# A gated attention and feed-forward decode kernel: the first weight matrix sent as eight transfers of sixteen rows

## The chip, the cores and the metric

The kernel runs on one core of a Trainium2 chip. The metric is the device time of one launch in microseconds. A core has five engines that matter here: TensorE (PE, with its weight loads shown as PEld), VectorE (DVE), ScalarE (ACT), GpSimd (POOL) and SyncE (SP), and sixteen DMA engines that move data between HBM and the on-chip memory SBUF. Data transfers are issued as instructions by SyncE and by ScalarE, each of which has a queue of its own; in the profile SyncE's is q1 and ScalarE's is q10. A transfer is cut into rows, one for each SBUF partition, and the rows are shared out over the DMA engines.

## The reference

Two tokens (batch 2, one position) of width 512 go through an attention block over a cache of 4096 positions and through a small feed-forward block; a gate mixes the two.

```python
x = A_x                                                   # [2, 1, 512]
g = sigmoid((x * gate_w).sum(-1, keepdims=True))
# attention: 32 heads of 128, K and V cache [2, 32, 4096, 128], bf16
q = (x @ wq)                                              # wq [512, 4096]
p = softmax(q k^T * 128 ** -0.5)                          # per head
a = (p v) @ wo                                            # wo [4096, 512]
# feed-forward
b = relu(x @ w1) @ w2                                     # w1 [512, 1376], w2 [1376, 512]
return g * a + (1 - g) * b
```

Everything is in bf16. The K cache and the V cache are 67 MB each; wq and wo are 4 MB each, w1 and w2 1.4 MB each.

## The kernel before, in words

The kernel is a list of instructions per engine, written out by hand. `sp(...)`, `act(...)`, `pe(...)`, `dve(...)` and `pool(...)` append one instruction to that engine's list together with what it waits for: `waits` names markers that other engines signal, `dwaits` names semaphores of transfers with the value to reach. A transfer adds 16 to its semaphore when all of it has landed. `emit` (lines 77 to 92) turns the lists into instructions, waits first.

*Where the data lies.* A large buffer `kv` has three regions (`NREG`) of 32,768 bf16 in each of 128 partitions. K and V are each cut into eight units of 8 MB; a unit fills one region, 64 KB in each partition. The units are sent in a fixed order (lines 185 to 188): five K units, then V and K by turns, then the remaining V. Each unit goes into the region that the unit three places before it has left, so from the fourth unit on SyncE waits, before it issues, for TensorE to be done with that earlier unit (lines 237 to 251). The third region first holds the small weights: wq (32 KB in each partition), w1 behind it (11,008 B in each partition: partition p holds rows 4p to 4p+3 of the matrix, which lie together in HBM), an identity matrix, and x with gate_w (lines 155 to 159). The third K unit is therefore sent only when the projection of x is done (the marks pe_qh, dve_setup and act_q).

*The first transfers.* ScalarE issues x and gate_w (lines 233 and 234), SyncE issues w1 and wq (235 and 236) and then the K units (250). The w1 transfer has 128 rows, one for each partition.

*The work behind them.* `gate` (line 282) transposes x and gate_w on TensorE and makes the gate's factors on ScalarE and VectorE. `x_proj` (line 340) waits for wq and w1 together (line 371) and multiplies x by both; its results are q, and the hidden layer before its ReLU. For each K unit VectorE transposes the region in place (`k_turn`, line 397) and TensorE multiplies by the block of queries that GpSimd has made (`w_block`, 388). `sm_max`, `sm_exp` and `sm_turn` make the softmax of a batch of four units; `spread` (442) puts the weights of one V unit in place on GpSimd, `v_go` (455) hands TensorE a token when the unit has landed, and `v_extract` (462) takes the result out. These loops run on TensorE as real loops with registers (`main_loop`, 476).

*The end.* Behind the last V unit SyncE issues w2 (line 252) and wo in four parts (255), so these are the last to arrive. ScalarE sends a rest of w2, `w2_lo`, 96 rows of 1 KB, between two V units (663). `project_first` multiplies the hidden layer by w2, `project` (615) the attention result by wo as its parts land; a copy on VectorE and one on ScalarE take the result to SBUF, and SyncE stores it (257).

*Fillers and the split of the lists.* `fill(name, n)` (609) appends n instructions that only add to a semaphore nobody waits for; they lengthen an engine's instruction list. Line 688 puts five of them on ScalarE, between the last small result and the final copy. Line 700 says how many instructions of each engine's list are emitted before TensorE's list, the rest after it: for SyncE four (w1, wq and two K units), for ScalarE two (x and gate_w).

Of the kernel before, what the change touches and what calls it, by code (L numbers as in the profile page):

```python
# [94 lines left out]
def bass_gated_mix__gqa_block_cached__dense_activation_relu__decode_kernel(  # L95
# [61 lines left out]
    w1_sb = kv[:, C, 16384:21888]  # L157
# [16 lines left out]
    def psf(p0, p1, c0, n):  # L174
        return PSF[p0:p1, c0:c0 + n]
# [4 lines left out]
    sem = {n: nc.alloc_semaphore("sem_" + n) for n in names}  # L180
# [16 lines left out]
    def freed(what):  # L197
        kind, u = what
        return f"pesc_{u}" if kind == "k" else f"pe_v_{u}"

    def sp(fn, waits=(), dwaits=()):
        P.add("sp", fn, waits=waits, dwaits=dwaits)
# [4 lines left out]
    def dve(fn, waits=(), signal=None, dwaits=()):  # L207
        P.add("dve", fn, waits=waits, signal=signal, dwaits=dwaits)

    def act(fn, waits=(), signal=None, dwaits=()):  # L210
        P.add("act", fn, waits=waits, signal=signal, dwaits=dwaits)

    def pe(fn, waits=(), signal=None, dwaits=()):
        P.add("pe", fn, waits=waits, signal=signal, dwaits=dwaits)
# [17 lines left out]

    act(lambda e: e.dma_start(x_sb[0:2], A_x.rearrange("b s d -> (b s) d")).then_inc(sem["x"], 16))
    act(lambda e: e.dma_start(x_sb[2:3], gate_w.rearrange("(o d) -> o d", o=1)).then_inc(sem["gw"], 16))
    sp(lambda e: e.dma_start(w1_sb, B_w1.rearrange("(p t) f -> p (t f)", t=4)).then_inc(sem["w1"], 16))
    sp(lambda e: e.dma_start(wq_sb, A_wq.rearrange("(p t) n -> p (t n)", t=4)).then_inc(sem["wq"], 16))
    for n, what in enumerate(order):
        if n >= NREG:
            waits = [freed(order[n - NREG])]
        else:  # L240
            waits = ["pe_qh", "dve_setup", "act_q"] if n == C else []
        if what == ("v", 7):
            c0 = 0
            for i, k in enumerate(LASTV):
                c1 = c0 + k * 4096
                sp(lambda e, n=n, c0=c0, c1=c1, i=i: e.dma_start(kv[:, n % NREG, c0:c1], unit_in(("v", 7))[:, c0:c1]).then_inc(sem["v7" + "ab"[i]], 16),
                   waits=waits if i == 0 else [])
                c0 = c1
        else:
            sp(lambda e, n=n, what=what: e.dma_start(kv[:, n % NREG, :], unit_in(what)).then_inc(sem_reg[n % NREG], 16),  # L250
               waits=waits)
# [50 lines left out]
    def r_(e, name):  # L302
        if name not in reg:
            reg[name] = e.alloc_register(name)
        return reg[name]

    def by_reg(e, ap, name):
        x = e.lower_ap(ap)
        n = reg[name].name
        return mybir.RegisterAccessPattern(ap=x.ap, dtype=x.dtype, memsetref=x.memsetref, regref=n, is_regloc_offset=False,  # L310
                                           reg_ap_offset=n, const_ap_offset=0, const_sub_tensor_id=0)

    def mm(e, dst, lhsT, rhs, cols=128, at=0, load=True):
        return e.add_instruction(mybir.InstMatmult(  # L314
            name=nc.get_next_instruction_name(), engine=mybir.EngineType.PE, ins=[rhs, lhsT], outs=[e.lower_ap(dst)],
            start_tensor_calc=False, stop_tensor_calc=False, tile_size=(128, cols), tile_position=(0, at),
            bass_skip_group_check=True, ldweights=load))

    def clear(e, dst, n, stop=False):
        return e.matmul(dst, lhsT=nil, rhs=nil.unsqueeze(1).to_broadcast([32, 4, 128]) if n == 512 else nil[:, 0:n],  # L320
                        start=not stop, stop=stop, tile_position=(0, 0), skip_group_check=True)

    def addresses(e, base, offs, first):
        for k, o in enumerate(offs):
            e.reg_add(r_(e, f"a{first + k}"), r_(e, base), o)
# [4 lines left out]
    def enter(name, parent=None, engines=(mybir.EngineType.PE,)):  # L330
        parent = nc.bb_map[parent] if parent else nc.cur_bb
        if open_block:
            open_block.pop().__exit__(None, None, None)
        b = nc.body(name, parent=parent, valid_engines=list(engines))
        b.__enter__()
        open_block.append(b)
# [3 lines left out]
    def x_proj():  # L340
        wqv = wq_sb.rearrange("p (t u a x) -> p t a u x", t=4, u=4, a=4)
        place_of = [(96 + r, 10, 128) for r in range(10)] + [(0, 1, 96)]

        def fn(e):
            for half in range(2):
                clear(e, psf(0, 128, V_C0 + BANK * half, BANK), 512)
            clear(e, psf(0, 128, H_C0, 2 * NF), 2 * NF)
            e.reg_mov(r_(e, "rm"), at["kv"] + 2 * C * REG)
            e.reg_mov(r_(e, "rh"), at["kv"] + 2 * (C * REG + 16384))
            e.reg_mov(r_(e, "rw"), at["zero"] + 4 * 636)  # L350
            e.reg_mov(r_(e, "p"), 0)
            e.br("x_pass")
            enter("x_pass")
            addresses(e, "rm", [2 * (256 * a + 2048 * half) for a in range(4) for half in range(2)], 0)
            addresses(e, "rw", [2 * 31], 8)
            addresses(e, "rh", [2 * (row + (m - 1) * n) for row, n, m in place_of], 9)
            for a in range(4):
                for half in range(2):
                    mm(e, psf(32 * a, 32 * a + 32, V_C0 + BANK * half, BANK), by_reg(e, xT32[:, 0, :], "a8"),
                       by_reg(e, wqv[:, 0, a, 2 * half:2 * half + 2, :], f"a{2 * a + half}"), 32, 32 * a, load=not half)  # L360
            for ft, (row, n, m) in enumerate(place_of):
                mm(e, psf(0, m, H_C0 + 2 * ft, 2), by_reg(e, w1_sb[:, row:row + (m - 1) * n + 1:n], f"a{9 + ft}"),
                   by_reg(e, xT32[:, 0, 0:2], "rw"))
            e.reg_add(reg["rm"], reg["rm"], 2 * 4096)
            e.reg_add(reg["rh"], reg["rh"], 2 * DFF)
            e.reg_add(reg["rw"], reg["rw"], 2 * 32)
            e.reg_add(reg["p"], reg["p"], 1)
            e.br_lt(reg["p"], 4, on_true="x_pass", on_false="x_done")
            enter("x_done")
            return clear(e, psf(0, 128, H_C0, 2), 2, stop=True)  # L370
        pe(fn, dwaits=[(sem["wq"], 16), (sem["w1"], 16)], waits=["act_xT"], signal="pe_qh")
        qt = ptm[:].rearrange("p x c h -> p (x c h)").bitcast(f32)
        dve(lambda v: v.transpose(out=qt.rearrange("p (n q) -> p n q", q=32).rearrange("p (y e) q -> p y e q", e=2),  # L373
                                  in_=PSF[:, V_C0:V_C0 + 1024].rearrange("p (y q e) -> p y e q", q=32, e=2)),
            waits=["pe_qh"], signal="dve_qt")
        act(lambda a: a.activation(out=q_sb[:].rearrange("p b u h k -> p b (u h k)"),
                                   in_=qt.rearrange("p (n x) -> p x n", x=32)[:, 0:2], func=ACT.Copy),
            waits=["dve_qt"], signal="act_q")
# [191 lines left out]
    def busy(n):  # L570
        pe(lambda e: mm(e, psf(0, 128, V_C0, n), e.lower_ap(X2[:, 0:128]), e.lower_ap(X2[:, 0:n])))
# [37 lines left out]
    def fill(name, n, dwaits=()):  # L609
        if name not in P.fill:  # L610
            P.fill[name] = nc.alloc_semaphore("fill_" + name)
        for i in range(n):
            P.add(name, lambda e: e.sem_inc(P.fill[name], 1), dwaits=(dwaits if i == 0 else ()))
# [30 lines left out]
    hint_here()  # L644
    gate()
    x_proj()
    w_block(0)
    w_block(1)
# [36 lines left out]
    busy(256)  # L685
    o_place()
    busy(512)
    fill("act", 5)
    fill("dve", 3)
    fill("pool", 3)  # L690
    fill("pool", 4, [(sem["wo2"], 16)])
# [5 lines left out]

    P.resolve()

    rest = (("sp", nc.sync, 4), ("act", nc.scalar, 2), ("pool", nc.gpsimd, 4), ("dve", nc.vector, 0))  # L700
    for name, eng, n in rest:
        P.emit(name, eng, 0, n)
    P.emit("pe", nc.tensor)
# [31 lines left out]
```

## Time and profile before

| | us |
|---|---|
| median of 3 runs | 342.68 (342.61 to 342.92) |
| the profiled execution | 342.64 |
| its span, first to last event of the profile | 341.3 |
| busy: TensorE, VectorE, GpSimd, ScalarE | 209.9, 155.4, 41.8, 13.9 |
| DMA packets, of these under 512 B | 3580, 405 |
| w1, issue to landing | 5.8 |
| wq, issue to landing | 15.0 |
| K units, issue to landing, median | 35.4 |

Times in the profile are microseconds from the start of the span. The time of an execution is 1.3 us longer than its span; forecasts are made for the time. In the DMA row of the page each digit is the mean busy share of the sixteen DMA engines in one of forty slices, in tenths, 9 for 90% or more. In the chain of waits one reads, in order of time, the work that the end waited for. In a timeline a name with q behind it (SPq, ACTq) is an engine's issue of a transfer; the number behind the start is how long the issue took, or, for several in one line, how long they took with the gaps between them. A transfer's packets are its rows, and for each DMA engine that it used one more of 4 bytes that counts up the semaphore. On q1 the rows of all its transfers are 3074 and the 4-byte packets 386, together the 3460 of the queue table.

### The profile page before, as it was taken

To read this page: it belongs to the slowest core of one execution; us is meant where nothing else is said; L and a number is where in the kernel's file an instruction comes from. 1 tells how busy PE (TensorE), PEld (TensorE's weight loads), DVE (VectorE), ACT (ScalarE), POOL (GpSimd) and SP (SyncE) were. 2 spreads that over 40 slices of the span, in tenths; PEclk is the share of its full clock that TensorE was granted. 3 is DMA by queue.
4 is the path that set the end of the run, shared out by engine and by line. 5 is a ranking of instruction groups with operands and counts; after the bars stand their busy time and mean duration, and the time that the engine had idled before them with its cause. 6 is when DMAs were issued, how large, how long until landed. Compare 5 with 4: busy or idle time off the path is not lost. (4 is left out here: it accounts for less than half of the span.)

```text
span 341.3 us, 3101 instructions
## 1 busy us (share of the span) xinstructions
PE 209.9 (61%) x1243; PEld 33.9 (10%) x843; DVE 155.4 (46%) x45; ACT 13.9 (4%) x37; POOL 41.8 (12%) x53
## 2 busy tenths in 40 slices
PE   0080079685968909972995059820993773718387
PEld 0040011000100101110111001100100100101024
DVE  1010897979799769229800693019805000000111
ACT  2001000000000020000000000000003000000000
POOL 1000000000000004005002300050000235050400
PEclk9999999999898965996799559965696659676789
DMA  8998989898999999998989898989999999999896
GB/s 346 434 492 369 492 369 492 369 492 369 492 392 468 399 461 445 415 484 376 492 369 492 369 492 369 492 369 492 392 468 392 468 438 424 398 441 461 374 440 264
DMA packets 3580, 145.46 MB, mean 426 GB/s; under 512 B 405, under 2 KB 634, under 8 KB 762
## 3 DMA queue, kind: packets, MB, share of 16 engines
q1 hardware_dynamic: 3460, 145.33, 98.7%
q10 hardware_dynamic: 118, 0.10, 0.1%
q8 instruction: 1, 0.02, 0.0%
q14 instruction: 1, 0.01, 0.0%
HBM read 145.43 MB, written 0.00 MB: 426 GB/s over the span
## 5 line engine op out<-in xcount | busy, mean ns | idle before, releaser
L404 DVE STREAM_TRANSPOSE kv<-kv 128x8192 uint32<-128x8192 uint32 (+1 forms) x17 | 138.6, 8186 | 74.4 <-DMA kv<-in_A_k_cache_dram 74.4
L314 PE MATMUL PS<-kv,zero 128*128 (+1 forms) x544 | 130.3, 421 | 40.4 <-PEq L481 40.4
L314 PE MATMUL PS<-kv,ptw 128*32 x512 | 48.1, 469 | 11.7 <-issue 11.5
L320 PE MATMUL PS<-zero 32*128 32x512 bf16 (+2 forms) x21 | 9.7, 537 | 57.6 <-ACT zero L410 20.3
L449 POOL TENSOR_TENSOR ptw<-E,mask 128x512 bf16<-128x512 bf16 x32 | 32.2, 1038 | 21.1 <-PE PS L314 10.9
L467 DVE TENSOR_TENSOR X<-PS,maskc 128x512 f32<-128x512 f32 x2 | 1.4, 692 | 64.1 <-PE PS L314 64.1
L314 PEld LDWEIGHTS PS<-kv,zero 128*128 (+1 forms) x144 | 13.6, 103 | 154.6 <-issue 154.6
L393 POOL TENSOR_TENSOR zero<-q_sb,mask 128x32 bf16<-128x32 bf16 x8 | 1.9, 251 | 147.0 <-PE PS L314 123.3
L471 POOL TENSOR_TENSOR X<-X,maskc 128x512 f32<-128x512 f32 x6 | 6.2, 1039 | 109.2 <-ACT X L470 109.2
L314 PE MATMUL PS<-X,zero 128*64 128x512 f32 x16 | 11.6, 819 | 12.3 <-PEq L481 12.3
L314 PEld LDWEIGHTS PS<-kv,ptw 128*32 x512 | 8.7, 99 | 50.4 <-issue 49.7
L320 PEld LDWEIGHTS PS<-zero 32*128 32x128 bf16 x21 | 2.1, 109 | 69.4 <-issue 43.7
L373 DVE STREAM_TRANSPOSE ptw<-PS 128x1024 f32<-128x1024 f32 x1 | 1.3, 1251 | 16.4 <-PE PS L320 16.4
L415 DVE TENSOR_REDUCE zero<-PS 128x2 f32<-128x2048 f32 x2 | 4.5, 2271 | 9.1 <-PE PS L314 9.1
L470 ACT ACTIVATE X<-PS 128x512 f32<-128x512 f32 x6 | 3.6, 597 | 71.4 <-PE PS L314 71.4
L422 ACT ACTIVATE nrow<-mmax 128x32 f32<-128x32 f32 x2 | 0.5, 228 | 132.8 <-DVE mmax L419 132.8
L440 DVE STREAM_TRANSPOSE E<-E 128x2048 bf16<-128x2048 bf16 x2 | 4.6, 2300 | 2.4 <-ACT E L430 2.4
L410 ACT ACTIVATE zero<-zero 1x1 f32<-1x1 f32 x9 | 1.8, 200 | 84.9 <-DMA kv<-in_A_v_cache_dram 67.9
L430 ACT ACTIVATE E<-PS,negm 128x1024 bf16<-128x1024 f32 x4 | 4.4, 1109 | 0.6 <-DVE negm L426 0.6
L284 PE MATMUL PS<-kv 3*128 3x3 bf16 x4 | 0.3, 165 | 6.5 <-DMA kv<-in_gate_w_dram 6.5
L598 PE MATMUL PS<-kv,oW 128*2 128x256 bf16 x64 | 4.0, 272 | 0.4 <-DMA kv<-in_A_wo_dram 0.4
L314 PEld LDWEIGHTS PS<-X,zero 128*64 (+1 forms) x16 | 1.8, 161 | 15.8 <-issue 15.6
(49 smaller groups left out, 27.6 us busy)
## 6 DMA issues: line engine op xcount, KB each, us to landing
kv<-in_A_v_cache_dram SPq DMA_DIRECT2D x1, 6144.0 KB, 36.7
kv<-in_A_wq_dram SPq DMA_DIRECT2D x1, 4096.0 KB, 15.0
kv<-in_A_wo_dram SPq DMA_DIRECT2D x1, 2560.0 KB, 35.9
kv<-in_A_v_cache_dram SPq DMA_DIRECT2D x1, 2048.0 KB, 41.3
kv<-in_B_w_dram SPq DMA_DIRECT2D x1, 1376.0 KB, 5.8
kv<-in_B_w_dram SPq DMA_DIRECT2D x1, 1280.0 KB, 30.1
kv<-in_A_wo_dram SPq DMA_DIRECT2D x1, 1024.0 KB, 37.9
kv<-in_A_wo_dram SPq DMA_DIRECT2D x1, 384.0 KB, 38.4
```

Source lines behind the costliest of these rows:

```text
L314: return e.add_instruction(mybir.InstMatmult(name=nc.get_next_instruction_name(), engine=mybir.EngineType.PE, ins=[rhs, lhsT], outs=[e.low ...
L320: return e.matmul(dst, lhsT=nil, rhs=nil.unsqueeze(1).to_broadcast([32, 4, 128]) if n == 512 else nil[:, 0:n], start=not stop, stop=stop, ...
L393: pool(lambda g: g.tensor_tensor(out=out, in0=q, in1=msk, op=ALU.mult), waits=([["act_q", "dve_mask8"], []] + [[f"pesc_{x}"] for x in rang ...
L404: ins = v.transpose(out=reg[:, 4096 * p0:4096 * p1], in_=reg[:, 4096 * p0:4096 * p1])
L410: return lambda a: a.activation(out=tick[:, 2 + i:3 + i], in_=tick[:, 0:1], func=ACT.Copy).then_inc(sem["go"], n)
L415: dve(lambda v: v.tensor_reduce(out=mpad[:, 0:2], in_=PSF[:, 0:2048].rearrange("p (x h q) -> p h x q", h=2, q=16), axis=AX.XY, op=ALU.max) ...
L430: act(lambda a, h=h: a.activation(out=E[:].rearrange("p (x h q) -> p h x q", h=2, q=16)[:, h], in_=PSF[:, 0:2048].rearrange("p (x h q) -> ...
L440: dve(lambda v: v.transpose(out=E[:], in_=E[:]), waits=[f"act_exp{b}"], signal=f"dve_et{b}")
L449: pool(lambda g, src=src, dst=dst: g.tensor_tensor(out=dst, in0=src, in1=msk, op=ALU.mult), waits=(([f"dve_et{b}"] if ub == 0 else []) + ( ...
L470: act(lambda e: e.activation(out=X2[:], in_=src, func=ACT.Copy), waits=[f"pe_v_{v}"], signal=f"act_x_{v}")
L471: pool(lambda e: e.tensor_tensor(out=X, in0=X, in1=msk, op=ALU.mult).then_inc(sem["xg"], 1), waits=[f"act_x_{v}"] + ([] if v else ["dve_se ...
L598: pe(lambda e, g=g: e.matmul(psf(64 * g, 64 * g + 2, FIN_C0, 256), lhsT=w, rhs=m[:, 256 * g:256 * g + 256], start=start, stop=stop, tile_p ...
```

## The change

w1 is sent as eight transfers in place of one. Transfer j takes the partitions j, j+8, j+16 and so on: sixteen rows of 11,008 B, one for each DMA engine. SyncE issues j = 0, 1, 3, 5 and 7, ScalarE j = 2, 4 and 6, behind x and gate_w. All eight count on the same semaphore, so TensorE now waits for 8 x 16 = 128. SyncE's wq and K units come behind its five transfers. ScalarE has three fillers fewer near the end, as many as it has transfers more. The split of the lists moves with the added instructions: eight of SyncE's and five of ScalarE's are emitted first.

```diff
     act(lambda e: e.dma_start(x_sb[2:3], gate_w.rearrange("(o d) -> o d", o=1)).then_inc(sem["gw"], 16))
-    sp(lambda e: e.dma_start(w1_sb, B_w1.rearrange("(p t) f -> p (t f)", t=4)).then_inc(sem["w1"], 16))
+
+    for j in range(8):
+        (act if j in (2, 4, 6) else sp)(lambda e, j=j: e.dma_start(w1_sb[j:128:8], B_w1.rearrange("(p t) f -> p (t f)", t=4)[j:128:8])
+                                        .then_inc(sem["w1"], 16))
     sp(lambda e: e.dma_start(wq_sb, A_wq.rearrange("(p t) n -> p (t n)", t=4)).then_inc(sem["wq"], 16))
...
-        pe(fn, dwaits=[(sem["wq"], 16), (sem["w1"], 16)], waits=["act_xT"], signal="pe_qh")
+        pe(fn, dwaits=[(sem["wq"], 16), (sem["w1"], 128)], waits=["act_xT"], signal="pe_qh")
...
-    fill("act", 5)
+    fill("act", 2)
...
-    rest = (("sp", nc.sync, 4), ("act", nc.scalar, 2), ("pool", nc.gpsimd, 4), ("dve", nc.vector, 0))
+    rest = (("sp", nc.sync, 8), ("act", nc.scalar, 5), ("pool", nc.gpsimd, 4), ("dve", nc.vector, 0))
```

## The prediction

> **What bounds the kernel.** I read the page's head and its row of DMA shares first, then the queue table, then the chain that ended last, then the timeline of the first 17 us, and at last the packet records of the trace, in which each DMA packet has a start, a duration, a size and a queue.
>
> ```profile
> span 341.3 us, 3101 instructions
> DMA  8998989898999999998989898989999999999896
> GB/s 346 434 492 369 492 369 492 369 492 369 492 392 468 399 461 445 415 484 376 492 369 492 369 492 369 492 369 492 392 468 392 468 438 424 398 441 461 374 440 264
> q1 hardware_dynamic: 3460, 145.33, 98.7%
> q10 hardware_dynamic: 118, 0.10, 0.1%
> HBM read 145.43 MB, written 0.00 MB: 426 GB/s over the span
> ```
>
> The sixteen DMA engines are busy in every slice; SyncE's queue (q1) alone holds 98.7% of their span. No engine of the core comes near (PE 61%, VectorE 46%). Packet by packet, each engine writes rows back to back: a 65,536 B row every 2.414 us in the K and V units, an 11,008 B row of w1 every 0.41 us. 145.43 MB over 16 engines at 65,536 B per 2.414 us is 334.9 us: nearly the whole span. So the kernel is one gapless stream per DMA engine, and whatever an engine loses at the start is still missing at the end, unless a gap later takes it up.
>
> ```profile
> 299.62 0.43 SPq L255
> 300.10 37.89 DMA kv<-in_A_wo_dram
> 337.99 0.04 issue
> 338.03 1.64 PE PS L598 x24
> 339.69 0.41 DVE ptw L623
> ```
>
> These are the last pieces of the chain of waits (start, length, what). The wo transfers are issued at 299.62 and wait 38 us behind what is already queued; only the last 24 matmuls, a copy and the output store stand behind the stream. The order of issue has room everywhere: the K and V units land no sooner than 24.7 us after their issue (the view of line 250) and need 8 rows x 2.414 = 19.3 of it on the engines, so at least 5.4 us of cover lie between an issue and its first row. There is no gap that could take up a loss, and none that a gain could open.
>
> ```profile
> 0.74 0.40 SPq L235 DMA_DIRECT2D kv<-in_B_w_dram  x1
> 0.74 0.54 ACTq L233 DMA_DIRECT2D kv<-in_A_x_dram  x1
> 1.19 0.42 SPq L236 DMA_DIRECT2D kv<-in_A_wq_dram  x1
> 1.31 0.23 ACTq L234 DMA_DIRECT2D kv<-in_gate_w_dram  x1
> 1.65 24.77 SPq L250 DMA_DIRECT2D kv<-in_A_k_cache_dram  x3
> 2.47 1.28 ACT L287 ACT_TABLE_LOAD   x1 [2.47 <-POOL zero L265]
> 6.53 0.26 PE L284 MATMUL PS<-kv 3*128 3x3 bf16 x4 [6.53 <-DMA kv<-in_gate_w_dram]
> 8.02 0.20 ACT L297 ACTIVATE gm<-gb 128x2 f32<-128x2 f32 x1 [0.23 <-DVE gb L296]
> 16.25 0.13 PEld L320 LDWEIGHTS PS<-zero 32*128 32x128 bf16 x2 [9.00 <-issue]
> ```
>
> This is the timeline of the start (start, length, what, idle before). The packet records beside it: w1's first rows start between 1.77 and 2.73 us on the sixteen engines and nine of them take 0.78 to 1.36 us in place of 0.41 (median over the sixteen 0.87); the second rows are nearly steady, the rest run at 0.413. The engines finish their eight rows between 5.58 and 6.13. Eight rows at 0.41 from 1.77 would end at 5.06, so this ramp costs the quickest engine 0.52 us and the slowest 1.07. The half microsecond between engines is still there in the landings of the last wo transfer (338.81 to 339.29). That ramp is all that a better start can win.
>
> **The change part by part, against the profiled execution's 342.64 us (its span 341.3 and 1.34 around it; the median of the runs shown is 342.68, 0.04 more).**
>
> SyncE issues five pieces, then wq and the K units. Issues on it follow each other by 0.45 us (0.74, 1.19, 1.65; four wo issues in 1.86). So wq goes out at about 0.74 + 5 x 0.45 = 3.0 in place of 1.19, k0 at 3.45, k1 at 3.9. From issue to first packet took 1.03 us (0.74 to 1.77): wq is on the engines at about 4.0, and they reach it no sooner than 5.06. Cost 0, covered by 1.0 us; k0 is needed at 15.27. The third K unit waits for q at 26.4 in any case, and its rows come after k1's, past 50 us.
>
> ScalarE issues three pieces behind gate_w, each some 0.35 us (line 663's issue; 0.23 and 0.54 on the two here): 1.57 to about 2.7. Its table load slips from 2.47 to 2.7 and has until 6.83. gate_w, now served at 5.60 behind seven w1 rows of its engine, has fewer rows ahead and may land some 2 us sooner; the gate's chain then ends before 8.02, and TensorE waits for wq until 16.25 anyway. Worth 0 either way, covered by 8 us.
>
> The pieces themselves: with both queues the last is issued at about 2.6 and is there at 3.6; an engine wants its eighth row at 4.64 at the earliest. Seven more semaphore packets per engine at 0.009 us: 0.06. Where an engine alternates between the two queues, w2_lo is the nearest row: with its 1 KB rows between them, the 64 KB rows take 2.447 against 2.420, so 0.027 for a switch, at most six: 0 to 0.16, and I take 0 because a switch lies beside waiting writes. One wait on 128 in place of 16 ends with the same last row. ScalarE's three fewer fillers stand in a stretch where it idles 5.2 us: 0. SyncE's four more instructions shift its code; nothing in the trace prices that, and I bound it by one issue (0.33) on either side and take 0.
>
> What is left is the price of a row, and here placement changes: a piece's sixteen rows go to every eighth partition, and all pieces take them in the same order. No row of the trace has this placement. From below: 0.41, the steady row, and no ramp: ends at 5.06, 1.07 us sooner. From above: every row costs the median first row, 0.872, from the late starters' 2.42: 2.42 + 6.98 + 0.06 + 0.16 = 9.62, 3.49 us later. Between them I take that two engines share one way into SBUF while their rows lie so: 2 x 0.41 = 0.82 per row, which is near the 0.872 of the only rows in this trace that belong to a transfer not yet streaming. 1.77 + 8 x 0.82 + 0.06 = 8.39 against 6.13: **+2.26 us**, 342.64 + 2.26 = **344.9**. The ramp is not added: a row that is written at half rate gives the reads time.
>
> [...]
>
> **The rivals.**
>
> *Every piece pays a start of its own.* For it: the slow first rows. Against it: wq's and k0's first rows, each of a new transfer, take 1.213 and 2.418 like all others, because they were queued behind a running one. Price: 8 x 0.872 + 0.06 from 1.77 ends at 8.81, +2.7: 345.3. It would show gaps or long rows without a pattern by engine.
>
> *The row stays at 0.41 and the ramp stays.* For it: sixteen engines stream at full rate in every layout that the trace shows, and 1 KB rows to 96 partitions took the same 0.046 us as those to 128. Against it: those rows are too short to queue up anywhere. Then +0.06 for the semaphores and 0 to 0.16 for switches: 342.7 to 342.9. "No change" is what a reader can't tell from the 342.68, under 0.2% or 0.7 us.
>
> *The ramp goes (the other side).* One mechanism: before, an engine's first row waits while 128 rows are handed out; x, two rows issued at the same 0.74, was on its engines at 1.67 and its rows took 0.044 at once. If sixteen rows are handed out eight times as fast, all engines begin at 1.7 and are never late. It decides only if a row stays at 0.41. The most it gives is 1.07 less 0.06: 341.6. Against it: nine engines had their first row by 1.96 and were slow all the same, as if the reads were late and not the hand-out.
>
> *The pieces don't spread over sixteen engines.* x with two rows used two engines (q10's 118 packets are 99 rows and 19 semaphores: 2 for x, 1 for gate_w, 16 for w2_lo), so a transfer of sixteen rows should use sixteen. Otherwise one engine would carry rows of its neighbours at 0.41 each, and the end moves out by several times that. I leave this under the dearer case.
>
> **How the numbers follow.** Shared ways 0.53 (343.4 to 346.0, by how far the two engines of a pair drift apart: engines half a microsecond apart now share less; with half the sharing undone it is 8 x 0.62, +0.7). A start for each piece, or fewer engines: 0.14. Unchanged rows: 0.19. The ramp gone: 0.14. So slower 0.67, same 0.19, faster 0.14. The range reaches from the whole ramp won, 341.7, to the bound above, 342.64 + 3.49 = 346.1; the forecast's own is 343.4 to 346.0.
>
> **What would show it.** q1 with 3476 packets, q10 with 214, 517 under 512 B in place of 405 (112 more semaphores): the change did what it says. w1 rows of 0.8 us on all engines, the last piece landing near 8.9 in place of 6.6, wq near 18.4 in place of 16.2, the first projection at 18.5 in place of 16.25, the last wo landing 2.3 us later, all else shifted by the same: the forecast. Rows of 0.41 with TensorE starting at 16.2 or sooner would make it wrong, and so would a shift at 16 us that is gone by 338, for then a later gap exists that I don't see.

## The result, and the profile after

The changed kernel takes 345.59 us in the median (345.48 to 345.96, six runs) against 342.64 us before (342.49 to 342.92, six runs): 2.95 us more, a ratio of 1.0087 with a 95% interval from 1.0074 to 1.0100. The forecast was 344.9, slower, with a range from 341.7 to 346.1. The profiled execution took 345.52 us.

The page of the changed kernel, its head, DMA queues and HBM row:

```profile
span 344.2 us, 3105 instructions
DMA packets 3692, 145.46 MB, mean 423 GB/s; under 512 B 517, under 2 KB 746, under 8 KB 874
q1 hardware_dynamic: 3476, 144.80, 98.0%
q10 hardware_dynamic: 214, 0.63, 0.8%
HBM read 145.43 MB, written 0.00 MB: 423 GB/s over the span
```

The same bytes go over the same engines in 2.9 us more. The packets are the ones forecast (3476, 214, 517), so each piece did use sixteen DMA engines: eight times sixteen rows, eight times sixteen counting packets.

The start of the changed kernel, from its timeline (start, length, what, idle before):

```profile
0.73 3.11 SPq L237 DMA_DIRECT2D kv<-in_B_w_dram  x5
1.60 1.90 ACTq L237 DMA_DIRECT2D kv<-in_B_w_dram  x3
3.60 1.28 ACT L290 ACT_TABLE_LOAD   x1 [3.60 <-issue]
3.86 0.26 PE L287 MATMUL PS<-kv 3*128 3x3 bf16 x4 [3.86 <-DMA kv<-in_gate_w_dram]
3.88 0.59 SPq L239 DMA_DIRECT2D kv<-in_A_wq_dram  x1
19.18 1.03 PE L323 MATMUL PS<-zero 32*128 32x512 bf16 x3 [13.78 <-DMA kv<-in_A_wq_dram]
27.30 1.25 DVE L376 STREAM_TRANSPOSE ptw<-PS 128x1024 f32<-128x1024 f32 x1 [21.26 <-PE PS L323]
38.57 8.71 DVE L407 STREAM_TRANSPOSE kv<-kv 128x8192 uint32<-128x8192 uint32 x1 [10.02 <-DMA kv<-in_A_k_cache_dram]
```

And the same two VectorE instructions of the kernel before, for the shift:

```profile
24.41 1.25 DVE L373 STREAM_TRANSPOSE ptw<-PS 128x1024 f32<-128x1024 f32 x1 [16.42 <-PE PS L320]
35.67 8.71 DVE L404 STREAM_TRANSPOSE kv<-kv 128x8192 uint32<-128x8192 uint32 x1 [10.02 <-DMA kv<-in_A_k_cache_dram]
```

The gate's inputs come 2.7 us sooner (3.86 in place of 6.53) and nobody gains by it. The query transpose is 2.89 us late, the first K unit 2.90 us late (38.57 against 35.67). The end of the chain of waits of the changed kernel:

```profile
303.31 37.56 DMA kv<-in_A_wo_dram
340.87 0.04 issue
340.91 1.62 PE PS L601 x24
342.53 0.02 issue
342.55 0.41 DVE ptw L626
```

The last matmuls start at 340.91 in place of 338.03: 2.88 late. Between 38 us and the end nothing is added and nothing comes back.

Where the 2.9 us arise is in the packet records. A record doesn't name its DMA engine, so the sixteen last w1 rows to end, the sixteen first wq rows and so on stand for the sixteen engines. Means over them, in us:

| | before | after | later by |
|---|---|---|---|
| last w1 row ends | 5.93 | 8.39 | 2.46 |
| first wq row behind it ends | 7.13 | 10.00 | 2.87 |
| last wq row ends | 15.59 | 18.49 | 2.90 |
| slowest engine starts its first K row | 15.82 | 18.62 | 2.80 |

A w1 row of 11,008 B takes 0.413 in the median before and 0.790 after; once the stream runs (rows that start after 6.2 us) it takes 0.824 to 0.852, all thirty-two of them. Two engines at this pace together write 2 x 11,008 B in 0.844 us, 26.1 GB/s; one engine alone wrote 11,008 B per 0.41 us before, 26.8 GB/s. So, by this estimate from the row times, two engines now get about what one had, as they should if they share one way.

### The profile page after: what moved, and what is told of

The parts are those of the page before. It is cut to its first block, busy times and chain, and to the rows that moved or that the text cites. A ratio compares the mean times of both kernels' runs of the same rounds, so it can differ in the third digit from the quotient of the medians.

```text
span 344.2 us, 3105 instructions
## 1 busy us (share of the span) xinstructions
PE 207.9 (60%) x1243; PEld 33.8 (10%) x843; DVE 155.4 (45%) x45; ACT 13.9 (4%) x37; POOL 41.8 (12%) x53
## 3 DMA queue, kind: packets, MB, share of 16 engines
q1 hardware_dynamic: 3476, 144.80, 98.0%
## 5 line engine op out<-in xcount | busy, mean ns | idle before, releaser
L317 PE MATMUL PS<-kv,zero 128*128 (+1 forms) x544 | 128.8, 417 | 42.6 <-PEq L484 42.6
L317 PEld LDWEIGHTS PS<-zero,kv 128*128 (+1 forms) x44 | 2.9, 158 | 3.5 <-issue 3.5
```

The lines of the kernel that those rows point to most:

```text
L317: return e.add_instruction(mybir.InstMatmult(name=nc.get_next_instruction_name(), engine=mybir.EngineType.PE, ins=[rhs, lhsT], outs=[e.low ...
```

## The experiments

Each kernel was timed beside the kernel before on the same chip. In the edits, `W` stands for `B_w1.rearrange("(p t) f -> p (t f)", t=4)`; the count that TensorE waits for, the fillers and the split of the lists follow the number of transfers.

**e1_sync_only: is it the turns between two queues?**

```diff
-        (act if j in (2, 4, 6) else sp)(lambda e, j=j: e.dma_start(w1_sb[j:128:8], W[j:128:8])
+        sp(lambda e, j=j: e.dma_start(w1_sb[j:128:8], W[j:128:8])
```

> All eight pieces go from SyncE, one queue. Shared ways by placement: w1's rows stay at 0.80 to 0.85 us, time 345.6 within 0.5. Rival, it is the alternation of two queues: rows go back to 0.41, w1 is then paced by SyncE's issues at 0.62 each, its last row ends near 6.6, time 342.9 to 343.4.

Measured: 345.54 us, 2.97 over before (ratio 1.0085, 1.0068 to 1.0102); rows that start after 6.2 us take 0.83 to 0.86. It is not the queues. Nor is it late issue: SyncE sends wq only at 5.78, behind the eight pieces, 1.9 us later than in the changed kernel, and the time is the same.

**e2_columns: eight transfers, but each over all partitions.**

```diff
-        (act if j in (2, 4, 6) else sp)(lambda e, j=j: e.dma_start(w1_sb[j:128:8], W[j:128:8])
+        (act if j in (2, 4, 6) else sp)(lambda e, j=j: e.dma_start(w1_sb[:, 688 * j:688 * j + 688], W[:, 688 * j:688 * j + 688])
```

> Eight transfers again, from the same two engines in the same turns, but each has all 128 partitions and an eighth of their bytes (1,376 B). Shared ways by placement: an engine writes 64 rows of about 0.06 us, w1 ends between 5.6 and 6.8, time 342.6 to 343.5. Rival, a price per small transfer (issue, semaphore, start of its own): as with the change, 345.3 to 345.8.

Measured: 343.94 us, 1.37 over before (1.0038, 1.0024 to 1.0052). Well below the change, but above what was expected. The median row takes 0.059; 64 x (0.059 - 0.052) = 0.45 us per engine is explained by that. The rest are mainly single rows, 38 of 0.28 to 1.32 us that start between 1.8 and 5.8 us; the earliest of them belong to the slow start that the kernel before has too, and for the others the runs show no cause.

**e3_blocks16: a denser placement.**

```diff
-        (act if j in (2, 4, 6) else sp)(lambda e, j=j: e.dma_start(w1_sb[j:128:8], W[j:128:8])
+        (act if j in (2, 4, 6) else sp)(lambda e, j=j: e.dma_start(w1_sb[16 * j:16 * j + 16], W[16 * j:16 * j + 16])
```

> Eight transfers of sixteen neighbouring partitions, same engines, same turns. Shared ways by placement: four engines share one way, a row takes 4 x 0.41 = 1.64, w1 ends near 15 in place of 8.7, time 352 within 1.5. Rival, a price per transfer, or a price for rows that lie apart in HBM: no slower than the change, 345.6 or less.

Measured: 349.62 us, 7.05 over before (1.0203, 1.0186 to 1.0220). Data rate during w1, the table of stretches (stretch; busy time by engine; TensorE's clock, DMA share, GB/s). Before:

```profile
1.70:6.20 4.50, 0.00 (x0) 0.00 (x0) 1.28 (x7) 1.28 (x1) 0.69 (x1) 1.00 1.12 430
```

e3_blocks16:

```profile
1.70:12.50 10.80, 0.53 (x8) 0.39 (x8) 1.45 (x8) 2.05 (x5) 0.69 (x1) 1.00 1.15 179
```

The DMA share stays full while the rate (packets are counted where they start, so a wq row at the edge is in it) falls from 430 to 179 GB/s: the engines aren't idle, each row takes longer, 1.385 us in the median of the later rows. Placement decides, since the transfers are as many and as large as in the change. The forecast of 1.64 per row and 352 missed, as too dear: 1.385 is 3.4 times 0.41, not 4 times. The four was an assumption of the author's that no run shows; the measured 3.4 stays without a cause.

**e4_order: the same pieces in another order.**

```diff
-    for j in range(8):
-        (act if j in (2, 4, 6) else sp)(lambda e, j=j: e.dma_start(w1_sb[j:128:8], W[j:128:8])
+    for n, j in enumerate((0, 4, 1, 5, 2, 6, 3, 7)):
+        (act if n in (2, 4, 6) else sp)(lambda e, j=j: e.dma_start(w1_sb[j:128:8], W[j:128:8])
```

> [...] Shared ways: two engines of a pair are out of step by some part of a row and so share less; a row takes 0.82 less that part, between 0.5 and 0.82, time 343.4 to 345.4, below the change. Rival, a price per transfer: the order doesn't matter, 345.6 within 0.2.

Measured: 345.09 us (344.80 to 345.82), 2.52 over before (1.0075, 1.0058 to 1.0092). In the median a row takes 0.688 in place of 0.790, and w1 ends at 7.71 in the mean in place of 8.39. The row times are the clear part, as a price per transfer would leave them alone; the time moves the same way, 2.52 over before in place of 2.95 or of the 2.97 of e1_sync_only, but its runs spread by 1.0. Why this order should lessen the sharing no run shows; what was measured is the shorter row.

**e5_two64: only the placement.** The edit against the kernel before:

```diff
-    sp(lambda e: e.dma_start(w1_sb, W).then_inc(sem["w1"], 16))
+    for j in range(2):
+        sp(lambda e, j=j: e.dma_start(w1_sb[64 * j:64 * j + 64], W[64 * j:64 * j + 64]).then_inc(sem["w1"], 16))
```

> [...] Shared ways: rows of 0.8 us, w1 ends at 8.0 to 8.4, time 344.8 to 345.6. Rival, the number of transfers or the stride in the partitions makes the loss: rows of 0.41, time 342.6 to 343.0.

Measured: 345.48 us, 2.92 over before (1.0087, 1.0070 to 1.0104). That 64 neighbouring partitions share as the change's pieces do was the author's assumption; a row takes 0.834 in the median, where it took 0.413 before. Its start, by the timeline:

```profile
19.18 1.03 PE L322 MATMUL PS<-zero 32*128 32x512 bf16 x3 [11.94 <-DMA kv<-in_A_wq_dram]
27.29 1.25 DVE L375 STREAM_TRANSPOSE ptw<-PS 128x1024 f32<-128x1024 f32 x1 [19.41 <-PE PS L322]
38.57 8.71 DVE L406 STREAM_TRANSPOSE kv<-kv 128x8192 uint32<-128x8192 uint32 x1 [10.03 <-DMA kv<-in_A_k_cache_dram]
```

Two transfers without a stride, without a second queue, reproduce the change to 0.01 us at each of these marks. So neither the number of transfers nor the stride nor the queues cost the 2.9 us. What the two kernels have in common is that each transfer has a part of the 128 partitions, and a row of about twice the time (0.790 and 0.834 in place of 0.413).

**e6_one_fill2: the tail alone.**

```diff
-    fill("act", 5)
+    fill("act", 2)
```

> w1 as one transfer again, but with two fillers on ScalarE in place of five: the changed tail alone. Both theories: the tail has no part, 342.6 within 0.3. If the tail's code had one, up to 0.3 of the 2.9.

Measured: 342.54 us against 342.56 (0.9999, 0.9989 to 1.0008). The fillers have no part.

**e7_halves and e10_quarters: more transfers and two queues, with all partitions.** In place of w1's one transfer, e7_halves has:

```diff
+    for j in range(2):
+        (act if j else sp)(lambda e, j=j: e.dma_start(w1_sb[:, 2752 * j:2752 * j + 2752], W[:, 2752 * j:2752 * j + 2752])
```

e10_quarters has four such pieces of 1,376 columns, odd ones from ScalarE.

> Two transfers with all 128 partitions, each half of every row (5,504 B), one from SyncE, one from ScalarE. Shared ways: none are shared, rows of 0.21, 342.6 to 343.1. Rival, two queues or two transfers cost by themselves: a part of the loss, 343.3 or more. A gain below 342.4 would mean that the hand-out of rows made the slow start.

> Four column pieces with all 128 partitions (2,752 B rows), by turns from SyncE and ScalarE. Shared ways: none are shared, so far below the change; with half as many rows as e2_columns the price of short rows is half: 342.8 to 343.4. Rival, a price for each transfer whatever its rows: half of the change's 2.9, 344.0 or more.

Measured: 342.51 us for e7_halves (1.0001, 0.9992 to 1.0011) and 342.54 for e10_quarters (1.0005, 0.9995 to 1.0014). Two or four transfers from two queues cost nothing that can be told, and win nothing. ScalarE's pieces don't stand ahead of wq here: their rows come by turns with wq's, and the last w1 row ends at 15.59 in e7_halves and 15.72 in e10_quarters, where it ended at 6.1 before. The last of these rows are counted at 18.44 in e10_quarters, so TensorE starts its projection 2.30 us later there, yet VectorE starts on the first K unit at 35.62, against 35.67 before. TensorE before:

```profile
16.28 1.03 PE L320 MATMUL PS<-zero 32*128 32x512 bf16 x3 [8.94 <-issue]
```

TensorE and VectorE of e10_quarters:

```profile
18.58 1.02 PE L323 MATMUL PS<-zero 32*128 32x512 bf16 x3 [13.86 <-DMA kv<-in_B_w_dram]
35.62 17.31 DVE L407 STREAM_TRANSPOSE kv<-kv 128x8192 uint32<-128x8192 uint32 x2 [7.67 <-DMA kv<-in_A_k_cache_dram]
```

A projection that starts this much later cost no time here; only what held up the stream of rows did.

**e8_wq_first: whose is the slow start?**

```diff
-    sp(lambda e: e.dma_start(w1_sb, W).then_inc(sem["w1"], 16))
     sp(lambda e: e.dma_start(wq_sb, A_wq.rearrange("(p t) n -> p (t n)", t=4)).then_inc(sem["wq"], 16))
+    sp(lambda e: e.dma_start(w1_sb, W).then_inc(sem["w1"], 16))
```

> wq ahead of w1, each one transfer. If the slow start belongs to the first reads whatever they are: the first wq rows take up to 1 us more than 1.21 and the time is 342.6 within 0.3. If it belongs to w1's short rows: the ramp goes, 341.6 to 342.2, faster than before.

Measured: 342.75 us against 342.56 (1.0001, 0.9991 to 1.0011). wq's first rows now take up to 2.36 us in place of 1.21, and w1's rows, later, all take 0.413. The slow start belongs to the first rows of the stream, whichever transfer they are of. The time is the kernel before's, as far as can be told.

**e9_columns_sync: e2_columns from one queue.**

```diff
-        (act if j in (2, 4, 6) else sp)(lambda e, j=j: e.dma_start(w1_sb[:, 688 * j:688 * j + 688], W[:, 688 * j:688 * j + 688])
+        sp(lambda e, j=j: e.dma_start(w1_sb[:, 688 * j:688 * j + 688], W[:, 688 * j:688 * j + 688])
```

> The eight column pieces (128 partitions, 1,376 B rows), all from SyncE. Price of short rows (0.059 us for 1,376 B, where 0.052 would be the rate of a long row): unchanged by the queue, 343.9 within 0.3. Rival, the turns between two queues made the 1.4 us of e2_columns: 342.7 to 343.3.

Measured: 345.38 us (344.79 to 345.85), 2.78 over before (1.0082, 1.0065 to 1.0098). Both expectations missed. The rows take 0.059 as in e2_columns, and thirteen engines start on the first K unit between 16.53 and 17.21 us, as there; three others are a microsecond behind, the last at 18.52 (17.29 in e2_columns, 15.82 before). The time follows the last engine. Why three fall behind stays open, and so does the better part of the price of eight column pieces.

**e11_wq_then_pieces and e12_wq_then_sync: was the slow start really beside the shared writes?** e11 is the change with wq's line ahead of the loop, e12 is e1_sync_only with the same move:

```diff
+    sp(lambda e: e.dma_start(wq_sb, A_wq.rearrange("(p t) n -> p (t n)", t=4)).then_inc(sem["wq"], 16))
     for j in range(8):
...
-    sp(lambda e: e.dma_start(wq_sb, A_wq.rearrange("(p t) n -> p (t n)", t=4)).then_inc(sem["wq"], 16))
```

> The change with wq ahead of the eight pieces, so that the pieces come in a running stream and the slow start falls on wq. If in the change the slow start lay beside the shared writes, as the prediction took it, both are now paid one after the other: w1 takes 6.6 to 6.8 us in place of 3.3 and the row behind it 0.4 more, time 346.0 to 346.7. Rival, they were paid one after the other already: 345.6 within 0.2.

> wq, then the eight pieces, all from SyncE, so that no piece mixes with wq's rows as in e11. If the slow start lay beside the shared writes in the change: it now falls on wq, w1 takes 6.6 to 6.8 us in place of 3.3 and the row behind it 0.4 more, 346.0 to 346.7, between e1_sync_only (345.5) and e11 (347.0). If start and sharing were paid one after the other already: as e1_sync_only, 345.5 within 0.3, and e11's excess was the mixing alone.

Measured: 347.03 us for e11 (346.78 to 347.37; 1.0129, 1.0113 to 1.0146) and 346.32 for e12 (345.99 to 346.45; 1.0108, 1.0091 to 1.0125). The time of e12 is 0.73 further over before than that of e1_sync_only (3.70 against 2.97; the two profiled executions differ by 0.46). Where the slow start falls on wq, it is paid as well, so in the change at least a part of it lay beside the shared writes. One part of e12's expectation missed: an engine's eight w1 rows add up to 6.0 us, not 6.6 to 6.8. That is what they add up to in the change, too (6.03). The row behind them did take 0.4 more, as expected: the first K row 2.83 in the mean in place of 2.42. e11 was expected no higher than 346.7. In it ScalarE's three pieces run among wq's rows, and these take 1.44 in the median in place of 1.21; that the mixing makes the 0.7 over e12 fits, but no run separates it.

## Why the prediction was right

*What bounds.* The kernel is one gapless stream per DMA engine, and a loss at its start reaches the end whole. That is the best supported point: in the runs below, those with no change of time included, the time goes with the moment at which the slowest engine starts on its first K row.

| | slowest engine later by | time over before |
|---|---|---|
| e7_halves | -0.22 | -0.05 |
| e6_one_fill2 | -0.15 | -0.02 |
| e10_quarters | -0.09 | -0.06 |
| e8_wq_first | 0.20 | 0.19 |
| e2_columns | 1.47 | 1.37 |
| e4_order | 2.44 | 2.52 |
| e9_columns_sync | 2.70 | 2.78 |
| the change | 2.80 | 2.95 |
| e5_two64 | 2.80 | 2.92 |
| e1_sync_only | 2.82 | 2.97 |
| e12_wq_then_sync | 3.10 | 3.70 |
| e11_wq_then_pieces | 4.39 | 4.43 |
| e3_blocks16 | 6.98 | 7.05 |

(The left column is from the profiled execution, the right from the medians; e12's profiled execution is its quickest, 345.99, 3.35 over the profiled execution before, and its longer first K rows come on top of the left column. e6_one_fill2 has nothing changed at the start and moves by 0.15, so about 0.2 in the left column says nothing.)

*The price of a row.* 0.82 was forecast; 0.824 to 0.852 is measured once the stream runs. That the rows' placement makes the price is what e3 and e5 show: 1.385 per row where rows lie in blocks of sixteen, the change's 2.9 us with nothing but two contiguous halves. That engines share ways *into SBUF* fits all of these, but it is argued: row p of w1 goes to partition p in every run, so no run parts where a row is written from where in HBM it is read. One support in the prediction was chance: it found 0.82 near the 0.872 of the first rows before, and e8 shows that those belong to the slow start. No run shows the forecast's term itself, two engines on one way; what the runs show in its place is the time of a row by the partitions of its transfer: 0.413 in the median with all 128 (before), 0.824 to 0.852 with every eighth once the stream runs (the change), 0.834 in the median with 64 neighbouring ones (e5_two64), 1.385 in the median of the later rows with sixteen neighbouring ones (e3_blocks16). Which two engines would make a pair was not seen, as the packet records don't name the engine.

*The size.* The sum gave +2.26 against 2.95. The step "1.77 + 8 x 0.82 + 0.06 = 8.39" put every engine's last w1 row at 8.39. The mean of the sixteen engines is 8.39, but that is luck, as two errors cancel. The start was later: the first packet came at 2.11 in place of 1.77, and the first rows of the other engines start up to half a microsecond behind it. The rows were cheaper: eight add up to 6.03 in place of 6.56, for 0.82 holds for the later ones, while those that start by 3 us take 0.64 in the median. The prediction's ground for leaving the ramp out, that shared rows give the slow reads time, is borne out as far as the first rows are no dearer here than the later ones; e12's eight rows, in a running stream, add up to as much. The forecast compares the slowest engines, and there the step was too small: 8.67 in place of 8.39.

The larger error is that the sum let the sharing end with w1. The first wq row behind it took 1.60 in the mean in place of 1.21, 0.4 us that the forecast doesn't have, and in e12 the first K row behind w1 paid the same 0.4. That w1's writes are still going on then is the author's reading of its last semaphores, which come 0.8 us behind the last packet (9.46 against 8.67; before, 6.59 against 6.14); it was not tried by itself. The engines come out of it closer together, 0.28 apart in place of 0.55, which gives 0.1 back at the slowest: 2.26 + 0.28 + 0.4 - 0.1 = 2.84, against the 2.80 of the table.

*What was costed at nothing.* The late wq: e1_sync_only, with wq later still, has the change's time. TensorE's wait for w1: in e10_quarters it ends 2.30 us later than before, and the time is that of the kernel before. The semaphores were not tried by themselves. The fillers: e6_one_fill2. The turns between the queues: e7_halves, e10_quarters. ScalarE's three issues took 1.90 us in place of some 1.1 and pushed the table load to 3.60, which then set the gate's first copy (4.89); with TensorE waiting for wq until 19.18 it cost nothing, as forecast.

*The rivals.* A price for each piece's own start is out as the cause of the 2.9 us, by e5 and e10; what eight column pieces cost beyond their row length (e2, e9) is open. The unchanged row is out by the rows themselves. The other side, that the slow start is the handing out of 128 rows, is not settled. In the change, with sixteen rows handed out first, the first packet came later, not sooner. But in e3_blocks16, where sixteen rows are handed out first as well, the sixteen first rows all start between 1.75 and 1.97 us, while before the last engine had its first row at 2.73; so a part of the late start may be the hand-out's. Against the rival the prediction says that nine engines had their first row by 1.96 and nine rows were slow; the records have eight engines by then, all slow, and ten slow rows in all, so the argument holds for those eight. None of the runs was faster than the kernel before by what can be told (e7_halves 0.9992 to 1.0011, e10_quarters 0.9995 to 1.0014).

## What to carry to other kernels

In a gapless load stream like this one, judge a transfer by the set of partitions that its rows reach at one time, not by its number of bytes or of rows: the pieces of e3_blocks16 and of the change are alike in both and cost 7.05 and 2.95 us. In this kernel 64 of the 128 partitions in a transfer cost 2.9 us on 1.4 MB (e5_two64), all of them in four transfers nothing that can be told (e10_quarters). To cut a load up, cut it along the row and not across the partitions, and into few pieces: four with rows of 2,752 B were free, eight with rows of 1,376 B cost 1.4 us from two queues and 2.8 from one. Whether the number of pieces or the length of the rows does this was not separated. And look at the slowest DMA engine at the first point where the stream is steady; here its delay there is that of the end within 0.2 us in twelve of the thirteen runs of the table above (e12_wq_then_sync: 0.6).

## What the runs showed of the hardware that was not expected

The issue of a piece took SyncE 0.57 to 0.60 us for sixteen rows eight partitions apart (one every 0.63) and 0.55 to 0.58 for 64 neighbouring rows, but 0.39 to 0.48 for sixteen neighbouring rows and 0.40 for 128. Where it was slow and w1 went first, the first packet came at 2.06 to 2.11 us in place of 1.74 to 1.77, and the wq issue behind it took 0.59 in place of 0.42. No run explains it. The late first packet is 0.34 us in the forecast's sum; the late issue of wq cost nothing.
